# Splitting the last output tile of an attention + MoE kernel into two 256-column halves, with the order of all instructions solved anew

## The chip, the cores and the metric

The kernel runs on one core of one Trainium2 chip. The metric is the device time of one launch in microseconds (us), so lower is better. Executions of one and the same kernel here scatter over about 2 us, so an effect of a few tenths is read from profiles, in which single instructions are timed to 0.01 us, and from the mean of several runs.

## The reference

```python
# attention: 8 batches, 8 heads, 576 tokens, head size 64
q_s = softmax(q, axis=-1);  k_s = softmax(k, axis=2)
kv  = einsum('bhsd,bhse->bhde', k_s, v)
x   = einsum('bhsd,bhde->bhse', q_s, kv)          # -> 4608 x 512
# MoE part: 4608 x 512 -> 4608 x 2048 -> 4608 x 512
h = x @ w_in;  g = where(h > 0, h, exp(min(h, 0)) - 1);  out = g @ w_out
```

## The kernel before

Each piece of work is an operation with a number, an engine and its dependences. A table, `ORDER`, lists for each engine the numbers in the order in which it runs them. The table was solved off line with a model of durations; the program then adds the waits that the dependences need, and fills modelled TensorE gaps with "spare" matmuls on the identity, which are meant to keep TensorE at full speed. It counts the spares itself, so their number changes with the order. Every engine runs its list strictly in order.

The tokens go in 9 blocks of 512. The first product (L543, "stream" below, after a start that prepares it) writes pairs of 128x512 tiles, ScalarE and VectorE turn them into `GT`, and the second product (L588) makes four 128x512 output tiles a block. In the names below W1 and W2 are `w_in` and `w_out`, QS is `q_s`, and ID is the identity. With ID TensorE transposes QS (L403), and a copy of that is `qsT`; L456 makes `kv`, L487 is the attention product, and its copy XT is what the first product reads. (Line numbers shift by some lines from kernel to kernel.) The parts that matter here, cut:

```python
def init(self):
    S.add("dve", 100, memset(self.ID, 0.0), W=["ID"])                  # operation 0
    S.add("gp", 300, affine_select(self.ID, ...), X=["ID"])            # operation 1, Pool; reads and writes ID
    self.ident = S.ops[-1]
...
# W1 on Pool's queue: not before the first K tile has landed (gate) and ID is made (ident)
self.load_w1(g0, g1, half, -30, [gate, self.ident] if half == 0 else ())
...
def out_store(self, jb, ts, bk, key):
    S.add("act", ..., activation(osb[:, :], self.bank(bk), AF.Copy))   # 128x512, PSUM -> SBUF
    for x in range(2):                                                 # two stores of 64 rows, 128 KB each
        q = "act" if x and gi == 8 * NBLK - 1 else "sp"
        S.add(q, ..., dma_start(rows[b, c], osb[x * 64:(x + 1) * 64, :]))
...
for ts in range(4):                                                    # the last block
    bk = 4 + ts % 2
    ...
    self.out_mm(NBLK - 1, ts, bk, jj0, jj1, key)                       # 16 matmuls of 512 columns
    self.out_store(NBLK - 1, ts, bk, key)
```

The softmax here doesn't subtract the row's maximum and nothing guards it: scores larger than these inputs give would overflow.

## Time and profile before

| | before |
|---|---|
| device time, median of 3 | 301.28 us (301.15 to 301.32) |
| span of the profiled execution | 300.0 us |
| TensorE busy | 286.4 us (95%) |
| start: until the unbroken stream of matmuls | 18.23 us |
| stream, first to last matmul's end | 278.1 us |
| tail: from the last matmul's end | 3.65 us |

The lines behind this table stand in the prediction. Read it as three stretches in a row: the start is a chain of loads and small work, the stream is TensorE without a gap worth naming, and the tail is one eviction and two stores. The start of the stream is taken as the start of the ninth W1 matmul: it is the first after a wait of 0.57 us.

### The profile page before, as it was taken

What the parts mean: (1) busy time and instruction counts of PE and PEld (TensorE: products, weight loads), DVE (VectorE), ACT (ScalarE), POOL (GpSimd) and SP (SyncE); (2) the same over time, 40 slices, a digit from 0 to 9 for tenths busy, and PEclk for the clock granted to TensorE, in tenths of its full rate; (3) what the DMA queues carried; (4) which work ended last, traced back from release to release, by engine and by line L of the source; (5) the groups of instructions that cost most, each with busy time, mean ns of one, the idle gap of its engine ahead of it and who ended that gap; (6) DMA issues with size and microseconds to landing.
All of it is one profiled execution on the core that took longest, in us unless ns stands there. A gap on an engine that the chain in (4) does not pass through costs nothing.

```text
span 300.0 us, 4412 instructions
## 1 busy us (share of the span) xinstructions
PE 286.4 (95%) x1849; PEld 235.0 (78%) x1849; DVE 189.3 (63%) x244; ACT 182.1 (61%) x211; POOL 21.7 (7%) x33
## 2 busy tenths in 40 slices
PE   1699999999999999999999999999999999999995
PEld 1578887677888888888888888888888888888883
DVE  3848944985898685894568855588437256655400
ACT  5758848998977967877755766534462423432411
POOL 0870145100000000000000000000000000000000
PEclk9999999999999999999999999999999999999999
DMA  7999998995488895289546326041311302004223
GB/s 269 394 373 391 391 390 261 249 320 198 117 264 241 125 342 189 66 268 273 169 116 164 90 78 171 2 101 40 81 43 45 72 0 52 0 0 107 56 60 95
DMA packets 35283, 49.96 MB, mean 167 GB/s; under 512 B 16320, under 2 KB 16320, under 8 KB 35264
## 3 DMA queue, kind: packets, MB, share of 16 engines
q1 hardware_dynamic: 29680, 34.09, 41.2%
q0 software_dynamic: 5504, 15.47, 16.1%
q8 instruction: 14, 0.23, 0.3%
q10 hardware_dynamic: 80, 0.13, 0.1%
q14 instruction: 5, 0.04, 0.0%
HBM read 36.70 MB, written 9.44 MB: 154 GB/s over the span
## 4 chain that ended last, share of the span: by engine, by line
PE 91%; DMA 5%; ACT 1%; POOL 1%; DVE 0%; SPq 0%; issue 0%
PE PS L588 44%; PE PS L543 43%; PE PS L487 3%; DMA W<-in_moe_w_in_dram 2%; DMA KR<-in_k_dram 2%; PE PS L456 2%; POOL W L332 1%; ACT ESB L559 1%; DVE GT L572 0%; ACT ESB L570 0%; PE PS L403 0%; SPq L315 0%; ACT OSB L605 0%
## 5 line engine op out<-in xcount | busy, mean ns | idle before, releaser
L588 PE MATMUL PS<-W,GT 128*128 128x512 f32 x576 | 141.1, 392 | 0.4 <-DVE GT L578 0.4
L543 PE MATMUL PS<-XT,W 128*128 128x512 f32 x576 | 140.5, 391 | 0.9 <-DMA W<-in_moe_w_in_dram 0.6
L543 PEld LDWEIGHTS PS<-XT,W 128*128 128x128 f32 x576 | 107.2, 188 | 24.1 <-DVE XT L512 1.4
L588 PEld LDWEIGHTS PS<-W,GT 128*128 128x128 f32 x576 | 106.8, 188 | 22.6 <-DVE GT L578 0.8
L559 ACT ACTIVATE ESB<-PS 128x1024 f32<-128x1024 f32 x72 | 73.7, 1027 | 65.9 <-PE PS L543 65.8
L576 DVE TENSOR_SCALAR ESB<-ESB 128x1024 f32<-128x1024 f32 x64 | 44.1, 691 | 67.3 <-ACT ESB L559 66.6
L578 DVE TENSOR_TENSOR GT<-ESB,PS 128x1024 fp32r<-128x1024 f32 x64 | 77.7, 1217 | 1.8
L605 ACT ACTIVATE OSB<-PS 128x512 f32<-128x512 f32 x32 | 18.8, 597 | 32.1 <-PE PS L588 32.0
L372 DVE TENSOR_REDUCE ZQ<-QR 128x18 f32<-128x1152 f32 x16 | 21.5, 1343 | 7.1 <-ACT QR L352 7.1
L509 ACT ACTIVATE XT<-PS 128x512 fp32r<-128x512 f32 (+6 forms) x32 | 19.5, 608 | 7.8 <-PE PS L487 7.3
L380 DVE TENSOR_TENSOR QS<-QR,RZQ 128x1152 f16<-128x1152 f32 x16 | 21.6, 1352 | 0.3
L352 ACT ACTIVATE QR<-QR 128x1152 f32<-128x1152 f32 x16 | 18.6, 1164 | 2.7 <-DMA QR<-in_q_dram 2.7
L356 ACT ACTIVATE KR<-KR 128x1152 bf16<-128x1152 f32 x16 | 18.5, 1161 | 2.7 <-DMA KR<-in_k_dram 2.7
L487 PE MATMUL PS<-qsT,MBLK 128*128 128x320 f32 (+5 forms) x64 | 14.2, 308 | 0.0
L487 PEld LDWEIGHTS PS<-qsT,MBLK 128*128 128x128 f32 x64 | 12.0, 194 | 2.6 <-DVE MBLK L469 0.2
L431 ACT ACTIVATE qsT<-QT 128x1152 fp32r<-128x1152 f16 x12 | 14.0, 1163 | 0.0
L365 ACT ACTIVATE VB<-VR 128x1152 bf16<-128x1152 f32 (+1 forms) x12 | 13.5, 1125 | 0.6 <-DMA VR<-in_v_dram 0.6
L572 DVE SCALAR_TENSOR_TENSOR GT<-PS,ESB 128x1024 fp32r<-128x1024 f32 x8 | 9.8, 1221 | 4.5 <-ACT ESB L570 4.4
L403 PE MATMUL PS<-ID,QS 128*128 128x128 f16 x36 | 3.7, 266 | 6.6 <-DVE QS L380 6.6
L469 DVE TENSOR_TENSOR MBLK<-PS,RZK 64x128 fp32r<-64x128 f32 x32 | 9.2, 289 | 0.9
L570 ACT ACTIVATE ESB<-ESB 128x1024 f32<-128x1024 f32 x8 | 8.5, 1059 | 0.2
L403 PEld LDWEIGHTS PS<-ID,QS 128*128 128x128 f16 x36 | 2.9, 122 | 7.2 <-DVE QS L380 6.9
(28 smaller groups left out, 58.7 us busy)
## 6 DMA issues: line engine op xcount, KB each, us to landing
out_dram<-OSB SPq DMA_DIRECT2D x63, 128.0 KB, 2.4
QR<-in_q_dram SPq DMA_DIRECT2D x12, 576.0 KB, 4.9
KR<-in_k_dram SPq DMA_DIRECT2D x12, 576.0 KB, 6.3
VR<-in_v_dram SPq DMA_DIRECT2D x12, 576.0 KB, 5.4
W<-in_moe_w_out_dram POOLq DMA_DIRECT2D x4, 1024.0 KB, 18.5
QR<-in_q_dram POOLq DMA_DIRECT2D x4, 576.0 KB, 11.2
KR<-in_k_dram POOLq DMA_DIRECT2D x4, 576.0 KB, 11.3
VR<-in_v_dram POOLq DMA_DIRECT2D x4, 576.0 KB, 8.0
```

The lines of the kernel that those rows point to most:

```text
L352: S.add("act", t_act(1152, False), lambda e: e.activation(flat(q), flat(q), AF.Exp), key - 3, X=[f"qR{i}"], follow=self.table)
L356: S.add("act", t_act(1152, False), lambda e: e.activation(ek[:, :, :, :].rearrange("p h c d -> p (h c d)"), flat(k), AF.Exp), key - 2, X=[ ...
L372: S.add("dve", t_dve(1152), lambda e: e.tensor_reduce(self.ZQ[i][:, :, :].rearrange("p h c -> p (h c)"), q[:, :, :, :].rearrange("p h c d ...
L380: S.add("dve", t_dve(1152), lambda e: e.tensor_tensor(qso, q[:, :, :, :], rz, ALU.mult), key - 3, R=[f"qR{i}", f"RZQ{i}"], W=[f"QS{self.al ...
L487: last = e.matmul(P[:, y:y + n_], M[:, f, :], T[:, c0:c1, f * 64:f * 64 + 64], start=True, stop=True)
L509: S.add("act", t_act((h1 - h0) * n_, True), lambda e, dst=dst, src=src: e.activation(dst, src, AF.Copy), key, W=W, X=X)
L543: last = e.matmul(P[:, t * 512:(t + 1) * 512], self.W1[:, kc, tt * 128:(tt + 1) * 128], self.XT[:, kc, rc:rc + BLK], start=(kc == 0), stop ...
L559: S.add("act", t_act(1024, True), lambda e: e.activation(esb[:, :], P[:, :], AF.Exp), key, W=[f"E{i}"], X=banks)
L576: S.add("dve", t_dve(1024, 2), lambda e: e.tensor_scalar(esb[:, :], esb[:, :], 1.0, -1.0, ALU.min, ALU.add), key, X=[f"E{i}"])
L578: S.add("dve", t_dve(1024), lambda e: e.tensor_tensor(gt, esb[:, :], P[:, :], ALU.max), key, R=[f"E{i}"], W=gw, X=banks)
L588: last = e.matmul(dst, GT[:, jj, ts * 128:(ts + 1) * 128], self.W2[:, jj, :], start=(jj == 0), stop=(jj == 15))
L605: S.add("act", t_act(512, True), lambda e: e.activation(osb[:, :], src, AF.Copy), key, W=[f"O{i}0", f"O{i}1"], X=[f"b{bk}"])
```

## The change

Its intent is a shorter tail: what follows the last matmul should be a 128x256 eviction and two 64 KB stores, and the other half of the tile is computed earlier, in another bank. Since operations were added, the whole table was solved again, so nearly every engine's order differs. The diff, with the tables cut, and the code shortened:

```diff
 ORDER, TensorE, end
-  ... 788 792 793 797 801 805
+  ... 788 792 793 805 797 801 809          # 805, 809: the two halves; 797, 801: the last two full tiles
 ORDER, VectorE, beginning
-  2 4 5 0 6 7 25 26 37 27 ...              # 0: zero ID; 25, 26: reduce, reciprocal;
+  4 5 2 6 7 25 26 0 27 37 ...              # 27: first QS product; 37: second reduction
 (all other lists differ too)

-    def out_mm(self, jb, ts, bk, jj0, jj1, key):
-        GT, dst = self.GT[jb % 2], self.bank(bk)
+    def out_mm(self, jb, ts, bk, jj0, jj1, key, c0=0, c1=512):
+        GT, dst = self.GT[jb % 2], self.bank(bk)[:, c0:c1]
 ...
+    def last_store(self, bk, osb, i, c0, c1, key):
+        S.add("act", t_act(n_, True), activation(osb[:, c0:c1], self.bank(bk)[:, c0:c1], AF.Copy), ...)
+        for x in range(2):
+            q = "act" if x and c0 else "sp"
+            S.add(q, ..., dma_start(rows[b, c][:, c0:c1], osb[x * 64:(x + 1) * 64, c0:c1]), ...)
 ...
-        for ts in range(4):
+        for ts in range(3):
 ...
+        for bk, c0 in ((0, 0), (5, 256)):
+            self.out_mm(NBLK - 1, 3, bk, 0, 16, key, c0, c0 + 256)
+            self.last_store(bk, self.OSB[i], i, c0, c0 + 256, key)
```

## The prediction

> **What bounds the kernel now.** I read the page first, for which engine sets the span; then the chain of waits that ended last, cut to the first 20 us and the last 26 us; then the timeline of both ends; then the landing times of single DMAs. From the page:
>
> ```profile
> span 300.0 us, 4412 instructions
> PE 286.4 (95%) x1849; PEld 235.0 (78%) x1849; DVE 189.3 (63%) x244; ACT 182.1 (61%) x211; POOL 21.7 (7%) x33
> L588 PE MATMUL PS<-W,GT 128*128 128x512 f32 x576 | 141.1, 392 | 0.4 <-DVE GT L578 0.4
> L543 PE MATMUL PS<-XT,W 128*128 128x512 f32 x576 | 140.5, 391 | 0.9 <-DMA W<-in_moe_w_in_dram 0.6
> L605 ACT ACTIVATE OSB<-PS 128x512 f32<-128x512 f32 x32 | 18.8, 597 | 32.1 <-PE PS L588 32.0
> ```
>
> TensorE is the bound: 1152 big matmuls, and the waits ahead of them add to 1.3 us. The mean of 392 ns is not a price, since matmuls overlap; start to start in the trace the 512-column ones are 227 ns apart. A table of busy time by stretch shows where TensorE is not full:
>
> ```profile
> 0.00:18.20 18.20, 8.81 (x123) 6.87 (x123) 10.55 (x22) 10.63 (x13) 9.97 (x20) 1.00 0.98 331
> 18.20:100.00 81.80, 81.29 (x578) 65.55 (x579) 62.36 (x79) 67.19 (x77) 11.78 (x14) 1.00 0.92 280
> ...
> 280.00:296.35 16.35, 16.31 (x72) 13.16 (x71) 3.05 (x3) 3.42 (x6) 0.00 (x0) 1.00 0.35 80
> 296.35:300.00 3.65, 0.00 (x0) 0.00 (x0) 0.00 (x0) 0.59 (x1) 0.00 (x0) 1.00 0.27 72
> ```
>
> First pair of figures after the stretch: its length and TensorE's busy time. So there are three parts: 18.2 us of start, 278.1 us of unbroken matmuls, 3.65 us of tail with no matmul. Only start and tail, and small bubbles in the middle, can give time. The chain of waits for the start, and the timeline of the tail:
>
> ```profile
> 1.75 6.67 DMA KR<-in_k_dram
> 8.42 0.30 issue
> 8.72 1.97 POOL W L332 x3
> 10.70 7.30 DMA W<-in_moe_w_in_dram
> 17.99 0.24 issue
> 18.23 1.86 PE PS L543 x7
> ```
>
> ```profile
> 296.35 0.60 ACT OSB L605
> ```
>
> ```profile
> 296.97 0.55 ACTq L615 DMA_DIRECT2D out_dram<-OSB  x1
> ```
>
> The stream begins when the second half of W1's first three groups lands (17.99 us); Pool issues that load, and may not before the first K tile lands (8.42). The tail is one eviction of 128x512 and two stores of 128 KB, issued together at 296.97 on the SP and ACT queues; they land at 299.28 and 299.57, 2.31 and 2.60 us later, the span ends at 299.96.
>
> **What the Trainium skill says.** "TensorE: Matmul & The Clock Gate", section "Back-to-back issue gap", gives a warm gap of N/2.4 + 2.5 ns: 216 ns at 512 columns, 109 at 256. The trace has the same slope with more fixed cost: 227 at 512, 175 at 384, 148 at 320, 119 at 256, so two half-width matmuls cost 238 against 227. At 192 it is 91, so no cliff shows near 256. "ScalarE: Activation LUTs", section "What ACT_TABLE_LOAD costs", gives 186 ns + 0.833 N for an ACTIVATE with immediates: 612 and 399 at 512 and 256. The trace has 597 for 512 and 392 for the one 128x256 eviction it has. "DMA: Bandwidth & Descriptors", section "Anatomy of one DMA — SWDGE (gpsimd) path", gives 2.0 us + bytes/436e9, fitted for the Pool path; for these SP and ACT stores it gives 2.30 us at 128 KB, and the trace has 2.31. "SBUF — State Buffer", section "Who interferes with whom", says that a VectorE instruction with two SBUF inputs and a GpSimd instruction that reads SBUF exclude each other for a whole instruction. The trace before can't show it: none of its four Pool casts meets such an instruction. I need it below.
>
> **The change, part by part.**
>
> *The tail.* The last 128x512 tile becomes two 128x256 tiles in two banks; the order of TensorE instructions shows the first half placed ahead of the last two full tiles, so only the second half comes last.
> - TensorE: 16 matmuls of 512 columns go, 32 of 256 come: 32 x 0.119 - 16 x 0.227 = 3.81 - 3.63 = +0.18 us, all on the path.
> - Last eviction: 256 instead of 512 columns, 0.392 - 0.597 = -0.205 us, on the path.
> - Last stores: 2 x 64 KB instead of 2 x 128 KB. The second store landed 0.29 us after the first, so 128 KB of store takes about 0.29 us; the last landing then comes 2 x 0.145 = -0.29 us earlier. Rows shrink from 2 KB to 1 KB; I take no cost for that.
> - Nothing takes their place: the last full tile ends 16 x 0.119 = 1.9 us before the end, its eviction takes 0.6, and SP issues its two stores in about 1.1 us (0.47 + 0.60 for the same pair before), so SP is free at 1.7, some 0.6 us before the last half needs it (1.9 + 0.4). The second half's bank was used by the tile two before, evicted 3 us earlier. The first half's eviction and stores lie inside full tiles.
> Sum of the tail: 0.18 - 0.205 - 0.29 = -0.32 us.
>
> *The start.* All other differences come from the order table. On VectorE the zeroing of ID (the identity, which Pool completes with a select that reads SBUF) moves from 1.19 us to just behind the reciprocal that ends at 7.41, and the first QS product (1.35 us, two SBUF inputs) moves ahead of the second reduction. QS is thus ready near 8.9 instead of 9.89. That gains nothing, because the stream waits for W1. But Pool's first W1 load waits for the select too. The select would start 0.24 us after the memset (as before: 1.30 to 1.54), near 7.75, when the QS product has just begun. If both exclude each other, it runs at 8.9 to 9.2, and the W1 issue goes from 8.72 to about 9.3, 0.6 us late. Pool's packets first moved at about 11.0 us, while the input loads drained till 11.4, so about 0.3 us of this is hidden under them: W1 and the stream come 0.3 us later. If they don't exclude each other, the select is done at 8.05, before 8.42, and nothing moves. I take half to two thirds of it: +0.2 us. TensorE's small work before the stream (8 matmuls done by 17.7 us) is rearranged, with the spare matmuls at other places; it had 0.57 us of wait before 18.23, and I expect it still to end before W1.
>
> *The middle.* The same instructions in another order. Adding every start-to-start distance over its usual value from 18 us on gives 3.6 us of bubbles in all; about 2.8 of these before 80 us, the largest 0.55 at 54.9 (a wait for GT). A new order can win or lose a part: I take 0 +- 0.6. Loads on Pool are also swapped (the third Q tile goes ahead of W2's first part, about 1.5 us at the 0.59 MB per 1.5 us seen); W2 landed at 27.35 and is first used at 31.4, so that is covered.
>
> Sum: -0.32 + 0.2 + 0 = -0.1 us.
>
> **The rivals.**
> 1. *The start slips by more.* For it: W1's chain has no slack at all, and the W1 load that lands at 17.99 took 2.1 us after the one before, the others 0.95 to 1.0, with the DMA rate down to about 220 GB/s from 16 to 17 us, so its landing is fragile. Against it: DMA work is conserved as long as the queues hold something. Time: 301.8 to 302.3.
> 2. *The new order closes bubbles.* For it: two true waits at 54.9 and 56.5 us cost 0.8 us. Against: most of the 3.6 us are switches between kinds of matmul, whose number the order hardly changes. Time: 300.0 to 300.5.
> 3. *The tail's gain is hidden or lost.* If the 64 KB stores land no earlier (1 KB rows, or the fixed part rules), only 0.18 - 0.205 = -0.02 remains, and the time is 301.4 with the start's slip.
> 4. *A stall by the early first half.* It needs a free bank (bank 0) and a third output buffer. The last pair of W1 groups is followed by two full tiles (7.3 us) ahead of it, while the ELU of a group took about 3 us after its matmuls. I give this little: +0.5 at most.
>
> **Range and chances.** 301.28 - 0.1 = 301.2. The middle's +-0.6, the start's 0 to +0.6 and the tail's -0.4 to 0 add to a range of 300.3 to 302.2. A change of 2% is 6 us: start and tail together hold 21.9 us, most of which no part of the change touches, and the middle has 3.6 us of bubbles. Faster by over 2% is practically impossible; slower needs a long stall that the order of instructions doesn't show. So 0.005, 0.985, 0.01.
>
> **What would show it.** In the profile after: 592 matmuls at L588, 32 of them 128x256, about 119 ns apart; a last eviction of 128x256 near 0.39 us; last stores landing about 2.2 to 2.3 us after issue; a stretch without matmuls at the end of about 3.15 us instead of 3.65. The first W1 load issued at 8.7 (no exclusion) or near 9.3 (exclusion, with the select starting when the QS product ends); the stream starting at 18.2 or 18.5. The prediction is wrong if the middle, from first to last matmul of the stream, differs from 278.1 + 0.2 by more than 0.6 us, or if the stream starts outside 18.0 to 18.8.

## The result, and the profile after

Before 301.35 us (median of 6, 301.15 to 302.42), changed 301.82 us (median of 6, 301.37 to 302.81). The ratio is 1.0012, with a 95% interval of 0.9992 to 1.0033: no change that the times can tell from none. A ratio, here and below, is the mean time of one kernel's runs over that of the other's of the same rounds, so it is not quite the ratio of the medians. All outputs are right.

In the profile the parts moved all the same. From the table of busy time by stretch of the kernel after (stretch, its length, then TensorE's busy time), cut at the end of its last matmul:

```profile
280.00:296.86 16.86, 16.85 (x90) 14.40 (x88) 3.33 (x4) 2.66 (x5) 0.00 (x0) 1.00 0.26 60
296.86:299.87 3.01, 0.00 (x0) 0.00 (x0) 0.00 (x0) 0.38 (x1) 0.00 (x0) 1.00 0.52 121
```

The stretch without matmuls fell from 3.65 to 3.01 us. The last instructions of the timeline after (start, length, engine, line, operation):

```profile
291.85 0.38 ACT L598 ACTIVATE OSB<-PS 128x256 f32<-128x256 f32 x1
...
296.89 0.38 ACT L598 ACTIVATE OSB<-PS 128x256 f32<-128x256 f32 x1 [1.31 <-PE PS L588]
297.30 0.47 SPq L605 DMA_DIRECT2D out_dram<-OSB  x1
297.30 0.55 ACTq L605 DMA_DIRECT2D out_dram<-OSB  x1
```

The reader sees two evictions of 0.38 us, the first long before the end, and the two last stores issued together, as before. They landed 1.93 and 2.21 us after issue; the 128 KB ones had taken 2.31 and 2.60. The 256-column matmuls came 120 ns apart in the trace.

The start went the other way. The chain of waits after, cut to the first 20 us (start, length, what):

```profile
7.46 0.09 DVE ID L292
...
7.78 1.24 POOL ID L293
...
9.31 1.97 POOL W L332 x3
11.29 7.29 DMA W<-in_moe_w_in_dram
...
18.82 1.38 PE PS L543 x5
```

Pool's select, which completes the identity, is now on the path. The timelines show why it took 1.23 us. First before, then after:

```profile
1.54 0.28 POOL L293 TENSOR_SCALAR_AFFINE_SELECT ID<-ID 128x128 f16<-128x128 f16 x1 [1.10 <-DVE VB L302]
```

```profile
7.42 0.11 DVE L292 MEMSET ID<- 128x64 uint32 x1
7.50 1.36 DVE L380 TENSOR_TENSOR QS<-QR,RZQ 128x1152 f16<-128x1152 f32 x1
7.78 1.23 POOL L293 TENSOR_SCALAR_AFFINE_SELECT ID<-ID 128x128 f16<-128x128 f16 x1 [7.33 <-DMA KR<-in_k_dram]
...
9.31 5.09 POOL L332 DMA_DIRECT2D W<-in_moe_w_in_dram  x8 [0.31 <-POOL ID L293]
```

The same select on the same tile takes 0.28 us early and 1.23 us beside the product, and it ends at 9.01, 0.16 us after the product's end (8.86). So the first W1 load is issued at 9.31, although K had landed at 7.60. Note that the releaser named in brackets is the K landing, which is only the last semaphore that the profile could name; what holds the select is inside its own bar. Spans on Pool are rough in this profiler, but those that wait for the select bear it out: TensorE's transposes start at 9.15 and the W1 issue at 9.31.

In all, against the first profile of before: start +0.59, stream -0.05 (with 0.2 more of matmuls in it), tail -0.63, so -0.1 us of span.

### The profile page after: what moved, and what is told of

Same layout as the page of the kernel before. It is cut to its first block, busy times and chain, and to the rows that moved or that the text cites. A ratio compares the mean times of both kernels' runs of the same rounds, so it can differ in the third digit from the quotient of the medians.

```text
span 299.9 us, 4457 instructions
## 1 busy us (share of the span) xinstructions
PE 286.7 (96%) x1871; PEld 236.1 (79%) x1871; DVE 189.4 (63%) x244; ACT 181.1 (60%) x212; POOL 22.9 (8%) x33
## 3 DMA queue, kind: packets, MB, share of 16 engines
HBM read 36.70 MB, written 9.44 MB: 154 GB/s over the span
## 4 chain that ended last, share of the span: by engine, by line
PE 93%; DMA 4%; POOL 1%; DVE 1%; ACT 1%; issue 0%; POOLq 0%
PE PS L588 44%; PE PS L543 44%; PE PS L487 3%; DMA W<-in_moe_w_in_dram 2%; PE PS L456 2%; DMA QR<-in_q_dram 1%; POOL W L332 1%; DVE ZQ L372 0%; POOL ID L293 0%; ACT QR L352 0%; PE PS L403 0%; ACT OSB L598 0%; DVE RZQ L376 0%; DVE ID L292 0%; POOLq L293 0%
## 5 line engine op out<-in xcount | busy, mean ns | idle before, releaser
L588 PE MATMUL PS<-W,GT 128*128 128x512 f32 (+1 forms) x592 | 140.8, 386 | 0.0
L588 PEld LDWEIGHTS PS<-W,GT 128*128 128x128 f32 x592 | 108.0, 188 | 21.9 <-DVE GT L572 0.7
L620 ACT ACTIVATE OSB<-PS 128x512 f32<-128x512 f32 x31 | 18.2, 597 | 28.4 <-PE PS L588 28.4
L356 ACT ACTIVATE KR<-KR 128x1152 bf16<-128x1152 f32 x16 | 18.5, 1162 | 0.3 <-DMA KR<-in_k_dram 0.3
L403 PE MATMUL PS<-ID,QS 128*128 128x128 f16 x36 | 3.1, 242 | 9.2 <-POOL ID L293 9.2
```

The lines of the kernel that those rows point to most:

```text
L356: S.add("act", t_act(1152, False), lambda e: e.activation(ek[:, :, :, :].rearrange("p h c d -> p (h c d)"), flat(k), AF.Exp), key - 2, X=[ ...
L588: last = e.matmul(dst, GT[:, jj, ts * 128:(ts + 1) * 128], self.W2[:, jj, c0:c1], start=(jj == 0), stop=(jj == 15))
L620: S.add("act", t_act(512, True), lambda e: e.activation(osb[:, :], src, AF.Copy), key, W=[f"O{i}0", f"O{i}1"], X=[f"b{bk}"])
```

## The experiments

All twelve were run in four calls, each on another chip; each call has its own runs of the kernel before. "Order of before" and "order of after" are the two tables.

| run | what it is | median us (n) | before | ratio (95%) |
|---|---|---|---|---|
| before_again | before | 301.79 (6) | 301.58 | 1.0004 (0.9982 to 1.0027) |
| before_split_ahead | order of before, split as in the change | 301.28 (6) | 301.58 | 0.9982 (0.9959 to 1.0005) |
| before_split | the same, both halves at the end | 301.10 (6) | 301.58 | 0.9986 (0.9960 to 1.0012) |
| after_id_first | after, ID zeroed first again | 302.01 (6) | 301.58 | 1.0004 (0.9977 to 1.0031) |
| before_id_late_product | before, ID late, product next | 303.22 (6) | 301.60 | 1.0052 (1.0032 to 1.0073) |
| before_id_late_reduce | before, ID late, reduction next | 301.45 (6) | 301.60 | 0.9993 (0.9975 to 1.0011) |
| after_whole_tile | order of after, no split | 302.64 (6) | 301.60 | 1.0037 (1.0018 to 1.0057) |
| after_again | after | 301.79 (6) | 301.60 | 1.0017 (0.9992 to 1.0042) |
| after_id_first_few_spares | after_id_first, at most 8 spares a gap | 301.71 (5) | 301.91 | 0.9989 (0.9971 to 1.0008) |
| after_few_spares | after, at most 8 spares a gap | 302.43 (6) | 301.91 | 1.0021 (0.9998 to 1.0044) |
| before_split_2 | before_split again | 300.94 (6) | 301.91 | 0.9975 (0.9956 to 0.9994) |
| after_id_first_2 | after_id_first again | 301.59 (6) | 301.91 | 0.9991 (0.9967 to 1.0015) |

And what their profiles show (one execution each, us; "K" is the landing of the first K tile, "issue" the first W1 load's issue, "4th" the landing of the fourth W1 load, "first" the first W1 matmul, "stream" the start of the stream, which is the ninth W1 matmul, "tail" the time from the last matmul's end to the end):

| profile | K | select | issue | 4th | first | stream | tail |
|---|---|---|---|---|---|---|---|
| before (first profile) | 8.42 | 0.28 | 8.72 | 17.99 | 15.09 | 18.23 | 3.65 |
| before_again | 8.27 | 0.28 | 8.57 | 16.75 | 15.19 | 17.66 | 3.65 |
| before_split | 7.68 | 0.28 | 7.98 | 16.69 | 14.89 | 17.35 | 3.04 |
| before_split_ahead | 7.72 | 0.28 | 8.02 | 16.45 | 15.14 | 17.55 | 3.02 |
| before_split_2 | 7.90 | 0.28 | 8.20 | 16.38 | 15.49 | 18.00 | 3.03 |
| before_id_late_reduce | 7.68 | 0.28 | 8.45 | 16.85 | 15.01 | 17.42 | 3.66 |
| before_id_late_product | 8.27 | 1.23 | 9.30 | 18.23 | 15.67 | 18.47 | 3.63 |
| after (first profile) | 7.60 | 1.23 | 9.31 | 18.58 | 15.74 | 18.82 | 3.02 |
| after_again | 7.87 | 1.24 | 9.58 | 17.84 | 16.63 | 19.07 | 3.02 |
| after_whole_tile | 7.73 | 1.23 | 9.44 | 17.29 | 16.41 | 18.87 | 3.58 |
| after_few_spares | 8.16 | 1.23 | 9.43 | 18.43 | 15.88 | 18.67 | 3.02 |
| after_id_first | 8.00 | 0.28 | 8.29 | 17.36 | 15.90 | 18.34 | 3.03 |
| after_id_first_2 | 8.22 | 0.28 | 8.52 | 16.94 | 16.29 | 18.73 | 3.03 |
| after_id_first_few_spares | 8.22 | 0.28 | 8.52 | 17.21 | 16.15 | 19.35 | 3.03 |

### The control: before, again

Edit: none.

> The kernel before, unchanged, as a control. In its first profile one of the 16 parts of the first K tile's load came late (landing 8.42 us, the pieces of the other 15 by about 7.6), in the changed kernel's profile the landing was 7.60. Theory 'straggler': that was chance, so this profile shows K landing near 7.6, Pool's first W1 load issued near 7.9, and the stream starting before 18.23 if W1's landing follows its issue, at 18.2 if the DMA's work alone sets it. Rival 'steady': K lands at 8.4 again and the stream starts at 18.2. Ratio to the kernel before 1.000 +- 0.002 by either; it gives the noise of the method.

K landed at 8.27, so not near 7.6; that part of "straggler" fell in this run. But the fourth W1 load landed at 16.75, and in all five later profiles of the order of before with an unhindered select between 16.38 and 16.85; only the first profile has 17.99. So its stream start of 18.23 was late by chance, and what usually starts the stream there is not W1. The chain of waits of this run:

```profile
14.80 0.41 PE PS L456 x35
15.21 1.15 PE PS L543 x4
16.35 0.52 PE PS L487 x2
16.88 2.21 PE PS L543 x9
```

No load of W1 stands in it, here or further up (it begins with the first load of Q): from 9.99 us on, TensorE's own small work runs through to the stream. The time ratio, 1.0004 with an interval of +-0.22%, is the noise of the method.

### The split alone, with the order of before

Edit (before_split_ahead): the split code, and the table of before with only its ends changed.

```diff
-TensorE  ... 793 797 801 805
+TensorE  ... 793 805 797 801 809
-ScalarE  ... 794 798 802 806 808
+ScalarE  ... 794 798 806 802 810 812
-SP       ... 790 800 795 799 796 803 804 807
+SP       ... 790 795 796 807 808 799 800 803 804 811
```

> The kernel before with its own order table, and only the last tile split, the first half ahead of the last two full tiles as in the change (the last few entries of the table are those of the change). Theory: the tail gives all its gain: 0.18 us more of matmuls, last eviction 0.38 instead of 0.60, last landing 2.2 us after issue instead of 2.6; from last matmul to end 3.05 instead of 3.65 us; time -0.4 us, ratio 0.9986. Rival: the landing is no earlier in the mean, ratio 1.000.

The tail fell to 3.02 us and the time by 0.18%. The theory held in the profile; by time its interval still reaches 1.0005.

Edit (before_split): the two halves in their natural place, 805 and 809 at TensorE's end, 807 808 811 at SP's.

> As before_split_ahead, but both halves at the end, one behind the other. Theory: the first half's stores are issued about 0.6 us before the matmuls end and land before the last ones need the queue; SP issues full tile, half, half one after the other (about 1.1 us per pair), and the last half's store on SP waits for SP by up to 1 us; last landing 0.3 to 0.8 us later than with the half ahead; ratio 0.999 to 1.002. Rival: SP's queue is free in time, ratio as with the half ahead, 0.9986.

The theory fell and the rival held: the last store was issued at once after the eviction and landed 2.24 us later; the tail is 3.04 us. The end of the timeline:

```profile
295.65 0.38 ACT L598 ACTIVATE OSB<-PS 128x256 f32<-128x256 f32 x1 [1.53 <-PE PS L588]
296.06 0.47 SPq L605 DMA_DIRECT2D out_dram<-OSB  x1
```

The second half's matmuls last 1.9 us, and SP issued the first half's pair in 1.1 us of that. Running the first half ahead of two full tiles buys nothing here that these profiles show.

### The late identity

Edits, VectorE's list in the table of before:

```diff
-2 4 5 0 6 7 25 26 37 27 ...
+2 4 5 6 7 25 26 0 27 37 ...    (before_id_late_product)
+2 4 5 6 7 25 26 0 37 27 ...    (before_id_late_reduce)
```

> The kernel before with one part of the change alone: ID is zeroed behind the first reciprocal on VectorE and the QS product (two SBUF inputs) follows it at once, as in the change; all other orders stay (the spare matmuls, which the program counts itself, become 10 and 8 instead of 12, 3 and 6). Theory 'exclusion': the select on Pool takes about 1.2 us instead of 0.28 and ends 0.1 to 0.2 us after the product; the first W1 load is issued at 9.3 us, whenever K lands; stream start 18.2 or later, where the kernel before has 17.4 to 17.7 in the three profiles in which W1's fourth load was not held up. Rival 'late select only': the select takes 0.28 us and W1 is issued 0.3 us after K's landing. By time: +0.6 us at most, ratio 1.000 to 1.003.

> As before_id_late_product, but what follows the zeroing on VectorE is the second reduction (one SBUF input), as in the order of the kernel before. Theory 'exclusion': nothing to exclude, so the select starts near 7.75 us and takes 0.28 us, W1 is issued 0.3 us after K's landing (7.9 to 8.7), the stream starts as in the kernel before (17.4 to 17.7). Rival 'the select is slow because DMA fills SBUF at that time, not because of VectorE': it takes about 1.2 us here too, and W1 is issued at 9.3.

The timeline with the product behind the memset:

```profile
7.48 1.36 DVE L379 TENSOR_TENSOR QS<-QR,RZQ 128x1152 f16<-128x1152 f32 x1
7.77 1.23 POOL L292 TENSOR_SCALAR_AFFINE_SELECT ID<-ID 128x128 f16<-128x128 f16 x1 [7.32 <-DVE ID L291]
```

and with the reduction behind it:

```profile
7.54 1.29 DVE L371 TENSOR_REDUCE ZQ<-QR 128x18 f32<-128x1152 f32 x1
7.86 0.28 POOL L292 TENSOR_SCALAR_AFFINE_SELECT ID<-ID 128x128 f16<-128x128 f16 x1 [7.42 <-DMA KR<-in_k_dram]
```

The select starts within 0.1 us of the same moment, under the same load traffic, and takes 1.23 us beside a VectorE instruction with two SBUF inputs and 0.28 beside one with a single input (the DMA moved 393 and 379 GB/s meanwhile). "Exclusion" held, and "DMA traffic slows the select" fell. In all five profiles with the product the select ends 0.15 to 0.16 us after it. That is less than its own 0.28, so some part of it was done before; that it stood still in between is the plainest reading, not measured. In time the product variant costs 0.52%, the reduction variant nothing (0.9993). Between the two lie 1.77 us of medians (303.22 - 301.45). That is more than the 0.6 us that I expected at most; the profiles explain 1.05 us of it (stream at 18.47 instead of 17.42, behind W1's fourth load). The profiled execution of the product variant was its fastest (302.23 of 302.23 to 304.20), so the usual one may be later still; no trace of one was taken, and the rest stays open. The two variants also differ in their spares, 18 in the trace of the product variant and 23 in the other (21 in before). In both variants they all run after the select, so they can't lengthen it, but a part of the difference in time may be theirs.

### The new order alone, and the changed kernel again

Edit (after_whole_tile): the code of before with the table of after, whose end reads 788 792 793 797 801 805 again. after_again has no edit.

> The changed kernel's new order table without the split: the last tile is one 128x512 tile at the end again. Theory 'the order costs what the split gives': from last matmul to end 3.65 us as before, stream start 18.3 to 18.8, time 0.4 us above the changed kernel and 0.5 to 0.8 above before, ratio 1.0015 to 1.003. Rival 'the order is neutral': ratio to before 1.000.

> The changed kernel, unchanged, beside the others on one chip. Theory: ratio 1.000 to 1.002, select about 1.2 us, W1 issued at 9.3, stream start 18.3 to 18.8, tail after the last matmul 3.03. If W1's loads were held up by chance in the first profile, the fourth lands near 17.2 here and the stream starts when the last XT copies are done, near 18.3, no earlier.

The new order without the split is slower than before by 0.37%, with an interval clear of 1. So "neutral" fell: the order costs about 1.1 us (0.5 to 1.7), more than the 0.5 to 0.8 that I expected and than the 0.4 to 0.75 that the split gives. The changed kernel came out at 1.0017, beside 1.0012 at first. In after_whole_tile the fourth W1 load landed at 17.29, no longer late, and the stream still started only at 18.87 (in after_again at 19.07); I had expected 18.3 to 18.8.

### Undoing the late identity in the changed kernel

```diff
-VectorE  4 5 2 6 7 25 26 0 27 37 ...
+VectorE  0 4 5 2 6 7 25 26 27 37 ...
```

> The changed kernel with one thing undone: the zeroing of ID is first on VectorE again; all other orders stay. Theory 'exclusion': Pool's select takes 0.28 us again instead of 1.23 and is done before 2 us, W1 is issued 0.3 us after K's landing (7.9 to 8.7, not 9.31), and the stream starts 0.6 us or more earlier than 18.82; time 0.6 us (0.2%) or more below the changed kernel, ratio to before about 0.998. Rival 'DMA work sets it': W1 is issued earlier but lands at 18.5 all the same, time as the changed kernel.

> after_id_first once more (the changed kernel with ID zeroed first), because its first timing, 1.0004 with an interval of 0.9977 to 1.0031, did not tell it from the changed kernel (1.0012 and 1.0017). Theory 'the late select costs about 0.5 us in this order too': W1 issued near 8.0 to 8.6, select 0.28 us, ratio 0.998 to 1.000. Rival 'the rest of the new start order binds just behind': first W1 matmul again near 15.9, stream start near 18.3, ratio 1.000 to 1.002.

The select is short again and W1 is issued 0.3 us after K in both. Yet the first W1 matmul came at 15.90 and 16.29 and the stream at 18.34 and 18.73, against 17.4 to 18.0 in the order of before (18.23 in its first profile, where W1 was late). The times were 1.0004 and 0.9991: a gain against the changed kernel is likely, but these intervals do not show it. Both sides of the first expectation fell: the stream came 0.48 us earlier than 18.82 and not 0.6, the ratio was not near 0.998, and W1's fourth load landed at 17.36, not at 18.5. The rival of the second expectation held for the start, its theory for the ratio (0.9991). The chain of waits of the first of the two:

```profile
9.01 1.14 PE PS L403 x9
...
11.21 0.64 PE PS L456 x33
11.86 1.93 PE PS L668 x17
13.78 0.75 PE PS L487 x2
...
14.55 0.69 DVE XT L512
15.25 0.61 DVE qsT L413
...
15.90 1.19 PE PS L543 x4
```

L668 are spare matmuls, 17 of them in a row on the path. I took them for the second cause and capped them:

```diff
-                count = int(idle / 80)
+                count = min(int(idle / 80), 8)
```

> The changed kernel with ID zeroed first again and with the spare matmuls capped at 8 per gap (8 and 8 in place of 10 and 17). In after_id_first the chain of waits ran through the 17 spare matmuls (1.93 us at the half clock) to the first attention product, the XT copies and the first matmuls of the stream at 15.90. Theory 'two causes, one behind the other': with both out of the way the product starts near 12.9 instead of 13.8, the first W1 matmul at 15.0 instead of 15.9, the stream at 17.4 to 17.6 as with the order of before; time 0.5 to 1 us below after_id_first, ratio 0.996 to 0.999. Rival 'the spares keep the clock up': the product and transposes run at the half clock for longer and eat the gain, first W1 matmul 15.5 or later, ratio 1.000.

> The changed kernel with ID late as in the change, and only the spare matmuls capped at 8. Theory 'two causes': W1, issued at 9.3 to 9.6 behind the select, now holds the stream alone: first W1 matmul near 15.0 to 15.5, stream start when W1's fourth load lands, 17.5 to 18.6, so a part of the gain at most; ratio 0.999 to 1.001. Rival 'spares alone': ratio as after_id_first_few_spares.

The theory fell. The chain of waits with ID first and few spares:

```profile
10.92 0.59 ACT qsT L410
11.51 1.05 ACT KR L356
12.56 0.50 ACT qsT L410
...
13.19 1.19 PE PS L487 x2
14.38 1.00 PE PS L403 x9
...
15.41 0.70 DVE qsT L413
...
16.15 1.96 PE PS L543 x4
```

The attention product did start earlier (13.19 instead of 13.78), but it took 1.19 us instead of 0.75, the nine transposes after it 1.00, and the first four W1 matmuls 1.96 us instead of 1.19: TensorE ran at about half speed for longer (the first W1 matmuls started 426 ns apart instead of 235, at a granted clock that the profile gives as 1.00 in both), so the rival held in this profile and the first W1 matmul came no earlier (16.15). With ID late (after_few_spares) the stream waited for W1's fourth load (18.43) as expected, but the first W1 matmul (15.88) and the time (1.0021) came later than expected. There, with the same cap, the first four W1 matmuls took 1.19 us again, so one profile each does not tell how often the cap slows them. What remains visible in both chains is the new order itself: on ScalarE the exponential of the second K tile (1.05 us) now stands between the two halves of qsT, and on TensorE the first attention product now stands ahead of the second set of transposes, whose copy (DVE qsT) therefore comes later. Neither was moved alone, so how much each costs stays open.

### The version that beats both

> The order of before with the split tile, both halves at the end, again, as the version that should beat both kernels. Theory: tail 3.03 us, stream start 17.4 to 17.7, ratio to before 0.9985 (0.44 us); below the changed kernel by 0.5 us or more.

The order of before with the split gave 0.9975 here (interval 0.9956 to 0.9994), 0.9986 and, with the half ahead, 0.9982: about 0.6 us under before, and below the changed kernel's 1.0012 and 1.0017 in each. That comparison goes through before; and only one of the three intervals is clear of 1 by itself. The stream start of 18.0 in this profile is outside the expected 17.4 to 17.7; TensorE's first W1 matmul was at 15.49.

## Why the prediction was right or wrong

The time was right: 301.82 us in a range of 300.3 to 302.2, and no change beyond noise was forecast. (The parts of that range, as stated, add to 302.5 at the top, not 302.2.) But the centre was 301.2, and that the time came this near is in part luck: the start missed by 1.0 us, beyond its own range of 0 to +0.6, and the middle gave some of it back. One of the prediction's own signs of being wrong appeared too, by a hair: the stream started at 18.82, outside 18.0 to 18.8 (and at 19.07 in after_again). Its three terms were not equally right.

**The tail, predicted -0.32 us: right in kind, a little small.** TensorE +0.18 (the halves came 120 ns apart, 119 predicted) and the eviction -0.21 (0.38 against 0.60; -0.205 predicted) held. The mis-sized term is the stores. I took the 0.29 us by which the second 128 KB store landed after the first as the time that 128 KB take, and halved it twice. In fact the distance within the pair stayed at 0.28 to 0.31 us with 64 KB, and both stores landed about 0.38 us earlier than their larger forerunners. So -0.39 instead of -0.29, and -0.45 us in all (3.65 to 3.02, less 0.18). The split alone, by time, gave -0.14 to -0.25%, which is 0.4 to 0.75 us.

**The start, predicted +0.2 us: the mechanism right, the size and one step wrong.** The mutual exclusion of product and select came as described: the select ended at 9.01 (8.9 to 9.2 predicted), W1 was issued at 9.31 (about 9.3 predicted). The term that failed is "about 0.3 us of this is hidden under them". Over the six profiles with the order of before and a short select, W1's first load is issued at 8.32 us and its fourth lands at 16.85 in the mean; over the five with the late select (one of them before_id_late_product) it is 9.41 and 18.07. So the landing came later by 1.2 us for an issue later by 1.1, and nothing shows as hidden; the prediction's argument that DMA work is conserved did not help. (Single profiles scatter: 7.98 and 16.69, but 8.57 and 16.75. That the first pair shows 0.59 both at the issue and at the stream is chance, since W1's fourth load was late in the first profile of before.) The step that failed is "TensorE's small work before the stream ... I expect it still to end before W1". That rested on one profile of before, in which W1's fourth load was late. In its other profiles the small work itself starts the stream, and the new order makes that work longer. Over the six profiles with the order of before and a short select the stream starts at 17.70 us in the mean (17.35 to 18.23), over the three with the start of the changed kernel (after, after_again, after_whole_tile) at 18.92 (18.82 to 19.07). So the start costs 1.2 us, not 0.2. The two with ID first and all spares stand at 18.34 and 18.73, so by these few profiles about 0.4 us of it is the late identity and 0.8 the rest of the new order. That QS was ready earlier gained nothing, as predicted.

**The middle, predicted 0 +- 0.6 us: inside, on the good side.** From the stream's start to its end, less the 0.18 us of the split where there is one, the means are 278.59 over the same six profiles with the order of before (278.07 to 279.06) and 278.19 over all seven with that of after (277.79 to 279.47): -0.4 us. The two ranges overlap, so a gain in the middle is likely but not shown. Some of that may be waits at fixed moments that a later start runs into less; it was not tested.

The sum by these means is 1.2 - 0.4 - 0.45 = +0.35 us, beside +0.12% and +0.17% measured, 0.4 and 0.5 us. **Of the rivals,** the first (the start slips by more, 301.8 to 302.3) is what happened, but its reason, a late W1 load, is only half of it: in after_again and after_whole_tile the load had landed (17.84 and 17.29) and the small work still kept the stream until 19.07 and 18.87, which no rival named. "The new order closes bubbles" may hold for those 0.4 us, and the start took them back; "the tail's gain is lost" and "a stall by the early first half" did not occur. So the expected gain of the change is real and is spent at the other end of the kernel, by an order that was solved for something else.

## What to carry to other kernels

When a change makes a solver redo a whole schedule, judge the edit and the new schedule apart: put the edit into the old schedule first, and diff what the solver moved at the start, where one late instruction on an idle engine can stand in front of the first load. Before naming the bound of a start-up phase, take a second profile; a load that happened to be late hides the chain that usually binds. And a wait that is shown inside an instruction's own bar (the same instruction, four times as long) is found only by comparing durations, not by the list of waits.

## What the Trainium skill lacked or had wrong

- "SBUF — State Buffer", section "Who interferes with whom": it was right; a Pool select of 0.28 us took 1.23 to 1.24 us when it started about 0.28 us into a 1.35 us VectorE product with two SBUF inputs, and 0.28 beside a reduction with one. It doesn't say how such a wait looks in a profile: the blocked instruction shows as busy, not as waiting.
- "DMA: Bandwidth & Descriptors", section "Anatomy of one DMA — SWDGE (gpsimd) path": 2.0 us + bytes/436e9 is fitted for DMAs issued by Pool, and the page has no such fit for stores issued by SP or ACT. Used for these, it fits a 128 KB store from SP (2.31 us) but not a 64 KB one (1.93 measured, 2.15 by the formula), nor the second of a pair issued at once, which landed about 0.3 us after the first at both sizes.
- "TensorE: Matmul & The Clock Gate", section "Back-to-back issue gap": the page calls N/2.4 + 2.5 ns the gap of isolated matmuls, and it is short of this kernel's spacing by 11 ns at 512 columns (227 against 216) and at 256 (120 against 109). The 131 ns that the page gives for 512 columns in a real kernel is far from the 227 of these f32 matmuls; the section doesn't say for which type it holds.
